# DeltaNet and a mixture of experts on one core: states summed in PSUM and copied by ScalarE, fewer residual and y banks, logits reduced one place later

## Chip, cores and metric

The kernel runs on one NeuronCore of one Trainium2 chip. The metric is the device time of one execution in microseconds (us), lower is better. The kernel before has a median of 526.48 us in 3 runs (524.97 to 529.17).

## The reference

Two layers, one after the other, all in float32. The first is a delta rule over 4 batches, 8 heads, 768 tokens and a head size of 48; the second sends each of its 3072 rows (8 heads x 48 = 384 numbers) through one of 8 experts.

```python
def _attn_ref(q, k, v, beta):
    k_n = k / (np.linalg.norm(k, axis=-1, keepdims=True) + 1e-06)
    state = np.zeros((B, H, D, D))
    for t in range(S):
        y[:, :, t] = np.einsum('bhd,bhde->bhe', q[:, :, t], state)
        v_old = np.einsum('bhde,bhd->bhe', state, k_n[:, :, t])
        state = state + beta[:, :, t] * np.einsum('bhd,bhe->bhde', k_n[:, :, t], v[:, :, t] - v_old)

def _moe_ref(x, w_gate, w1, w2):
    logits = x @ w_gate
    expert_idx = np.argmax(logits, axis=1)
    gate_w = softmax(logits)[np.arange(N), expert_idx]
    for e in range(E):
        mask = expert_idx == e
        out[mask] = gate_w[mask] * (np.maximum(x[mask] @ w1[e], 0.0) @ w2[e])
```

## The kernel before

**Chunks and steps.** The sequence of a batch is cut into 6 blocks of 128 tokens, so there are 24 chunks (block, batch), numbered n = 4 * block + batch. Within a chunk the delta rule is solved in four sub-blocks of 32 tokens. The main loop (L994) is a pipeline over both: step t works on sub-block 0 of chunk t, sub-block 1 of chunk t-1, sub-block 2 of chunk t-2 and sub-block 3 of chunk t-3, all four on the 128 partitions of one tile. It has 27 steps; a step is about 8 us long in the stretch that matters here.

**What a step issues, in this order.** `residual(t)`: TensorE forms in one PSUM bank `ks` what the state (L424) and the solved sub-blocks `u` (L436) predict for the 32-row values, and VectorE subtracts that from the values `v_all` (L443, called the subtraction below). Then, where there are any, four pairs of key products `pg` (L266). Then the last part of the chunk finished in the step before: TensorE forms the rows `xp` of x with their logits (L516), ScalarE copies the row to SBUF (L517), VectorE sums the logits `rl` (L518). Then `apply(t)`: 32 small matmuls of the subtracted values with the inverses `wt` of the sub-blocks (L451), written into the same bank `ks`, which ScalarE copies to `u` (L455, four copies). Then `finish(t-3)`: outputs `yp` from the state (L474), the chunk's key-value product `ku` (L483) which VectorE adds to the state tile `st` in SBUF (L487, two adds), the rest of `yp` (L492), and ScalarE's two copies `yt` (L496). Last, query-key products `pq` (L266), copied by ScalarE and masked by GpSimd (`pm`, L276 and L277). `scale_v(t+1)` scales the next values: on ScalarE for steps 4 to 19 (L404, eight instructions, one per head), on VectorE in the other steps (L407, one instruction).

**Work beside the path.** `beside(t, 0)` to `beside(t, 6)` stand between these parts. Each issues some instructions of the 32x32 inverses on VectorE (L384, L388), of weight splitting for the experts (L695), and of generators on the list `fine`, which give each finished row a slot in its expert's buffer. For chunks below 16 the generator is `pool_slots` (mostly GpSimd), from 16 on `emit_slots` (VectorE). It takes two chunks at a time: `rl` gives an arg-max mask `oh_all` (L635), TensorE counts rows before it with two constant matrices (`pp`, L639 and L642), ScalarE copies the counts (`ct`, L645), GpSimd makes slot numbers `sli` (L660) and issues two scattering DMAs to DRAM (`xg`, L666; in `emit_slots` L582 and L589). Each engine takes its instructions strictly in the order in which this loop issued them, so an instruction that waits holds up all that stands behind it on its engine.

**PSUM before.** The 8 banks are three of tag "y" (`yp`, `ku`, `xp`, `pp`, `db`), two of tag "ks" and three of tag "g".

**After the attention.** Expert 0's rows are read back from `xg` (`xr`, L731), transposed by TensorE (`xt`, L784) and sent through the two expert matmuls (L759, L770); the first of this begins inside the last steps of the loop, and from about 300 us on only the experts are left.

## Time and profile before

| | us |
|---|---|
| median of 3 runs | 526.48 |
| lowest and highest | 524.97, 529.17 |
| profiled execution | 525.89 |
| its span in the trace | 524.2 |

Times of the trace count from the start of the span; what lies outside it is 1.7 us. The mean granted TensorE clock of the span was 0.955. In a row of the trace "[0.64 <-DVE v_all L443]" means that the engine stood idle for 0.64 us before this instruction and that the named instruction released it. PE is TensorE, DVE VectorE, ACT ScalarE, POOL GpSimd, SP SyncE. In the windows, the granted clock is the third column from the right, 1.00 being 2.4 GHz.

### The profile page before, as it was taken

The page shows a single profiled execution, that of the slowest core. Times are in us where ns is not written, and L with a number is a line of the kernel's source. Part 1 is how long each engine was busy: PE and PEld are TensorE (multiplying, and loading weights), DVE is VectorE, ACT ScalarE, POOL GpSimd, SP SyncE. Part 2 cuts the span into 40 slices and gives each one's busy share as a digit, 9 for nine tenths or more (in the row PEclk, how much of TensorE's full clock was granted, in tenths as well). Part 3 has the DMA queues.
Part 4 walks back from the last instruction along what each step waited for, and adds up shares of the span by engine and source line. Part 5 has one row for each costly group of instructions (what it writes and reads, how often), then busy time and mean ns, then how long its engine had stood idle before and what let it go on. Part 6 is the DMA issues. An engine that isn't in the chain of part 4 may idle for free. (4 is left out here: it accounts for less than half of the span.)

```text
span 524.2 us, 17557 instructions
## 1 busy us (share of the span) xinstructions
PE 463.6 (88%) x7212; PEld 426.7 (81%) x7212; DVE 331.6 (63%) x996; ACT 269.5 (51%) x622; POOL 142.9 (27%) x305
## 2 busy tenths in 40 slices
PE   6866769899888888988789999999999999999995
PEld 4755658788776767777689889999999999999995
DVE  3989999698897689435654386636372827445330
ACT  2542236588676667755644246535354636354320
POOL 7002011465763655433130201020202020110202
PEclk9976689899999899898999999999999999999998
DMA  5878769569479557394442156555373636453001
GB/s 165 194 256 227 232 153 315 168 157 294 119 198 275 183 159 225 123 301 123 151 157 80 67 158 221 177 168 160 123 226 114 211 129 210 137 163 108 33 3 44
DMA packets 66060, 87.88 MB, mean 168 GB/s; under 512 B 26425, under 2 KB 50767, under 8 KB 65968
## 3 DMA queue, kind: packets, MB, share of 16 engines
q1 hardware_dynamic: 62512, 77.01, 50.2%
q0 software_dynamic: 3456, 9.57, 5.0%
q8 instruction: 67, 1.10, 0.9%
q14 instruction: 25, 0.20, 0.1%
HBM read 60.24 MB, written 23.56 MB: 160 GB/s over the span
## 5 line engine op out<-in xcount | busy, mean ns | idle before, releaser
L770 PE MATMUL y<-w2h,hx 128*128 128x384 f32 x352 | 93.8, 341 | 0.4 <-PEq L1143 0.4
L773 POOL DMA_INDIRECT out_dram<-yo,idx x32 | 30.7, 958 | 202.3 <-ACT yo L1116 129.8
L695 DVE TENSOR_TENSOR w2l<-w2r,w2h 128x768 fp32r<-128x768 f32 x32 | 31.2, 978 | 69.9 <-ACT w2h L694 69.7
L388 DVE TENSOR_TENSOR lw<-lw,tmp 128x84 f32<-128x84 f32 (+29 forms) x239 | 67.3, 316 | 0.4
L384 DVE TENSOR_TENSOR tmp<-lg,lw 128x84 f32<-128x84 f32 (+29 forms) x239 | 65.2, 307 | 2.5
L770 PEld LDWEIGHTS y<-w2h,hx 128*128 128x128 f32 x352 | 64.1, 188 | 0.7 <-issue 0.7
L455 ACT COPY u<-ks 32x384 f32<-32x384 f32 x96 | 45.1, 470 | 32.8 <-PE ks L451 30.3
L770 PE MATMUL y<-w2l,hx 128*128 128x384 f32 x176 | 59.4, 337 | 0.0
L759 PE MATMUL h<-xl,w1h 128*128 128x384 f32 (+1 forms) x168 | 57.5, 342 | 0.2 <-DVE xl L695 0.2
L759 PE MATMUL h<-xh,w1h 128*128 128x384 f32 (+1 forms) x168 | 57.5, 342 | 0.0
L759 PE MATMUL h<-xh,w1l 128*128 128x384 f32 (+1 forms) x168 | 57.4, 342 | 0.0
L762 ACT ACTIVATE hx<-h 128x448 fp32r<-128x448 f32 (+1 forms) x64 | 32.9, 518 | 33.1 <-PE h L759 32.3
L424 PE MATMUL ks<-st,kt 128*32 128x96 f32 x768 | 46.2, 257 | 2.4 <-issue 2.4
L1116 ACT ACTIVATE yo<-y,gt 128x384 f32<-128x384 f32 x21 | 12.2, 582 | 66.9 <-PE y L770 51.0
L763 DVE SCALAR_TENSOR_TENSOR hx<-h,hx 128x448 fp32r<-128x448 f32 (+1 forms) x64 | 36.9, 587 | 15.1 <-ACT hx L762 14.9
L277 POOL TENSOR_SCALAR_AFFINE_SELECT pm<-pm 128x1024 f32<-128x1024 f32 x24 | 26.6, 1110 | 71.2 <-ACT pm L276 68.6
L451 PE MATMUL ks<-v_all,wt 32*32 32x48 f32 x1536 | 25.7, 206 | 21.6 <-DVE v_all L443 18.9
L249 ACT COPY gg<-pg 128x512 f32<-128x512 f32 x48 | 25.8, 588 | 35.2 <-PE pg L266 35.2
L451 PEld LDWEIGHTS ks<-v_all,wt 32*32 32x32 f32 x1536 | 21.5, 107 | 26.0 <-DVE v_all L443 21.7
L424 PEld LDWEIGHTS ks<-st,kt 128*32 128x32 f32 x768 | 34.5, 113 | 5.8 <-issue 2.9
L266 PE MATMUL pq<-qt,kt 64*128 64x128 f32 x384 | 32.1, 299 | 2.3 <-issue 1.0
L695 DVE TENSOR_TENSOR w1l<-w1r,w1h 128x1024 fp32r<-128x1024 f32 x24 | 29.4, 1225 | 6.8 <-ACT w1h L694 6.8
(194 smaller groups left out, 987.9 us busy)
## 6 DMA issues: line engine op xcount, KB each, us to landing
w1r<-in_w_dram SPq DMA_DIRECT2D x24, 512.0 KB, 4.0
w2r<-in_w_dram SPq DMA_DIRECT2D x32, 384.0 KB, 3.7
kt<-in_kt_dram SPq DMA_DIRECT2D x24, 256.0 KB, 2.8
qt<-in_qt_dram SPq DMA_DIRECT2D x24, 256.0 KB, 5.8
xg<-zrow SPq DMA_DIRECT2D x7, 788.0 KB, 6.2
kg<-in_kt_dram SPq DMA_DIRECT2D x17, 256.0 KB
xr<-xg SPq DMA_DIRECT2D x7, 591.0 KB, 5.2
xn<-row SPq DMA_DIRECT2D x10, 394.0 KB, 5.1
```

Of the source, the lines that this page charges most:

```text
L266: nc.tensor.matmul(pg[a][:, p], lhsT=kt[r, p], rhs=xt[r, p], start=True, stop=True, tile_position=(64 * a, 0), skip_group_check=True)
L384: nc.vector.tensor_tensor(out=x, in0=lg[:, r0:r1, c:c + 1].broadcast_to([128, r1 - r0, b - a]), in1=lw[:, c:c + 1, a:b].broadcast_to([128, ...
L388: nc.vector.tensor_tensor(out=lw[:, r0:r1, a:b], in0=lw[:, r0:r1, a:b], in1=x, op=ALU.add)
L424: nc.tensor.matmul(ks[32 * q:32 * q + 32, 2 * p:2 * p + 2, :], lhsT=kt_t[n % KTL][:, p, 32 * q:32 * q + 32], rhs=st_view(n % B, p), start= ...
L451: nc.tensor.matmul(ks[r, h, :], lhsT=tiles[n // B]["wt"][r, n % B * H + h, :], rhs=vn[r, h, :], start=True, stop=True, tile_position=(32 * ...
L455: nc.scalar.copy(out=uview(n)[r], in_=ks[r])
L695: nc.vector.tensor_tensor(out=lo, in0=src, in1=hi.bitcast(F32), op=ALU.subtract)
L759: nc.tensor.matmul(ps, lhsT=w[:, d, fs], rhs=x_[:, d], start=(n == 0), stop=(n == len(terms) - 1))
L762: nc.scalar.activation(out=hh, in_=ps, func=AF.Relu)
L763: nc.vector.scalar_tensor_tensor(out=hl, in0=ps, scalar=0.0, in1=hh.bitcast(F32), op0=ALU.max, op1=ALU.subtract)
L770: nc.tensor.matmul(ps, lhsT=h(f)[h_], rhs=w2[w][:, f, :], start=(n == 0), stop=(n == len(terms) - 1))
L773: nc.gpsimd.indirect_dma_start(out=out, out_offset=bass.IndirectOffsetOnAxis(ap=idx, axis=0), in_=yo, in_offset=None, bounds_check=N - 1, ...
```

## The change

1. **States as running sums.** `ku` gets no bank of its own any more. Two PSUM banks `sum0` and `sum1` hold the sums of batches 0, 1 and 2, 3 through the whole loop; the matmuls of `ku` add onto them, and only the first ones of block 0 set the start flag. Where VectorE added `ku` to `st`, ScalarE now copies the sum to `st` (two copies of 48x192). The fourth `u` copy is issued ahead of them.
2. **Banks.** The two sum banks come from tag "ks" (2 to 1) and tag "y" (3 to 2). The tiles `db` of batches 2 and 3, used at the start, borrow the sum banks.
3. **Scaling.** `scale_v` runs on VectorE in steps 4 to 10 too; ScalarE keeps steps 11 to 19.
4. **Logits.** The reduction to `rl`, and with it the start of the slot generator, is issued behind `beside(t, 1)` instead of ahead of it. `xp` and the row copy stay where they were.

```diff
-    YB = 3
-    KSB = 2
+    YB = 2
+    KSB = 1
+    VA = 11
...
         if not last:
-            ku = pss.tile([112, NP, D], F32, name=f"ku{tb}_{b}", tag="y", bufs=YB)
+            if tb == 0 and b % 2 == 0:
+                sum_t.append(pss.tile([112, 2, NP, D], F32, name=f"sum{b // 2}", tag=f"sum{b // 2}"))
+            ku = sum_t[b // 2][:, b % 2]
...
                 nc.tensor.matmul(ku[64 * (h % 2):64 * (h % 2) + m, h // 2, :], lhsT=kn, rhs=u[:, h, :],
-                                 start=True, stop=True, skip_group_check=True)
+                                 start=(tb == 0 and b % 2 == 0 and h < 2), stop=True, skip_group_check=True)
             for a in range(2):
                 r = slice(64 * a, 64 * a + D)
-                nc.vector.tensor_tensor(out=st[r, :, r], in0=st[r, :, r], in1=ku[r], op=ALU.add)
+                nc.scalar.copy(out=st[r, :, r], in_=ku[r])
...
-        emit_x(n, yt, row[:, n % w], rl[:, n % w])
+        xp = emit_x(n, yt, row[:, n % w])
+        yield
+        nc.vector.tensor_reduce(out=rl[:, n % w], in_=xp[:, :, 2 * D:].rearrange("t p e -> t e p"), axis=AX.X, op=ALU.add)
         if n % w == w - 1:
             fine.append((pool_slots if n < PG else emit_slots)(tb, b - w + 1, w, row, rl))
...
         beside(t, 0)
         chunk(ks_, t)
         run(fin)
-        if t + 1 < NN + LAG and not B <= t < NN - B:
+        if t + 1 < NN + LAG and not VA <= t < NN - B:
             scale_v(t + 1)
         if t + 1 < NN:
             clear_u(t + 1)
         beside(t, 1)
+        run(fin)
         copies = apply(t)
...
         beside(t, 2)
+        run(copies)
         run(fin)
-        run(copies)
-
-        if B <= t < NN - B:
+
+        if VA <= t < NN - B:
             scale_v(t + 1, act=True)
```

**What moves on TensorE.** Step 14, the counting matmuls `pp` of two chunks and the rows `xp` (`ks`<-`u` is the end of the residual, `ks`<-`v_all` the start of apply). Before:

```order
L436 MATMUL ks_3311<-u_2594,gg_109 32x48
L639 LDWEIGHTS ltri
L639 MATMUL pp_0_3359<-oh_all,ltri 128x16
L642 LDWEIGHTS ones
L642 MATMUL pp_0_3359<-oh_all,ones 128x8
L642 LDWEIGHTS ones
L642 MATMUL pp_0_3359<-oh_all,ones 128x8
L642 LDWEIGHTS ones
L642 MATMUL pp_0_3359<-oh_all,ones 128x8
L516 MATMUL xp_2_3376<-esel,yt_2_3282 128x104 x4
L451 MATMUL ks_3311<-v_all,wt_2772 32x48 x3
```

After:

```order
L523 MATMUL xp_2_3303<-esel,yt_2_3224 128x104 x4
L646 LDWEIGHTS ltri
L646 MATMUL pp_0_3316<-oh_all,ltri 128x16
L649 LDWEIGHTS ones
L649 MATMUL pp_0_3316<-oh_all,ones 128x8
L649 LDWEIGHTS ones
L649 MATMUL pp_0_3316<-oh_all,ones 128x8
L649 LDWEIGHTS ones
L649 MATMUL pp_0_3316<-oh_all,ones 128x8
L454 MATMUL ks_3253<-v_all,wt_2714 32x48 x3
L454 MATMUL ks_3253<-v_all,wt_1905 32x48
```

`pp`, which waits for `oh_all`, stood ahead of `xp` and now stands behind it, right ahead of apply. In steps 6, 8 and 10 the key products `pg` stand between them too, and `pp` moves behind both.

**What moves on VectorE in a step.** Step 16, behind the subtraction: inverse work (`lw`, `tmp`), the logits `rl` and the adds to `st`. Before:

```order
L384 TENSOR_TENSOR tmp_14_3746<-lg_2583,lw_1933 128x51
L518 TENSOR_REDUCE rl_0_3765<-xp_0_3766 128x8
L388 TENSOR_TENSOR lw_1933<-lw_1933,tmp_14_3746 128x17x12
L388 TENSOR_TENSOR lw_1933<-lw_1933,tmp_14_3746 128x17x3
L384 TENSOR_TENSOR tmp_15_3777<-lg_2583,lw_1933 128x192
L384 TENSOR_TENSOR tmp_15_3777<-lg_2583,lw_1933 128x64
L388 TENSOR_TENSOR lw_1933<-lw_1933,tmp_15_3777 128x16x12
L388 TENSOR_TENSOR lw_1933<-lw_1933,tmp_15_3777 128x16x4
L384 TENSOR_TENSOR tmp_16_3835<-lg_2583,lw_1933 128x180
L384 TENSOR_TENSOR tmp_16_3835<-lg_2583,lw_1933 128x75
L487 TENSOR_TENSOR st_135<-st_135,ku_1_3838 48x4x48 x2
L388 TENSOR_TENSOR lw_1933<-lw_1933,tmp_16_3835 128x15x12
```

After:

```order
L387 TENSOR_TENSOR tmp_14_3686<-lg_2521,lw_1907 128x51
L391 TENSOR_TENSOR lw_1907<-lw_1907,tmp_14_3686 128x17x12
L391 TENSOR_TENSOR lw_1907<-lw_1907,tmp_14_3686 128x17x3
L387 TENSOR_TENSOR tmp_15_3701<-lg_2521,lw_1907 128x192
L387 TENSOR_TENSOR tmp_15_3701<-lg_2521,lw_1907 128x64
L511 TENSOR_REDUCE rl_0_3690<-xp_0_3691 128x8
L391 TENSOR_TENSOR lw_1907<-lw_1907,tmp_15_3701 128x16x12
L391 TENSOR_TENSOR lw_1907<-lw_1907,tmp_15_3701 128x16x4
L387 TENSOR_TENSOR tmp_16_3768<-lg_2521,lw_1907 128x180
L387 TENSOR_TENSOR tmp_16_3768<-lg_2521,lw_1907 128x75
L391 TENSOR_TENSOR lw_1907<-lw_1907,tmp_16_3768 128x15x12
L391 TENSOR_TENSOR lw_1907<-lw_1907,tmp_16_3768 128x15x5
```

The reduction `rl` stands four inverse instructions later, and the two adds to `st` are gone.

**What moves on VectorE late.** Step 22, the slot numbers `sli` of chunks 16 and 17 and the subtraction (`w1l` is weight splitting). Before:

```order
L574 TENSOR_REDUCE sl_all<-pos_0_4769 128x2
L582 CAST sli_0_4802<-sl_all 128x2
L695 TENSOR_TENSOR w1l_4612<-w1r_2_4468,w1h_4611 128x1024
L443 TENSOR_TENSOR v_all<-v_all,ks_4809 128x384
L518 TENSOR_REDUCE rl_2_4855<-xp_2_4856 128x8
L407 TENSOR_TENSOR v_all<-v_all,nt_all 128x384
```

After:

```order
L581 TENSOR_REDUCE sl_all<-pos_0_4714 128x2
L702 TENSOR_TENSOR w1l_4544<-w1r_2_4404,w1h_4543 128x1024
L446 TENSOR_TENSOR v_all<-v_all,ks_4740 128x384
L589 CAST sli_0_4782<-sl_all 128x2
L410 TENSOR_TENSOR v_all<-v_all,nt_all 128x384
L511 TENSOR_REDUCE rl_2_4786<-xp_2_4787 128x8
```

The cast to `sli` stood ahead of the weight split and the subtraction, and now stands behind both.

On ScalarE the two `st` copies stand behind the four `u` copies of each step and ahead of the eight scalings and the `yt` copies.

## Rows read from the trace of the kernel before

**Rows 1.** Windows of the span: PE busy (count), PEld, DVE, ACT, POOL, clock, DMA

```profile
60.00:80.00 20.00, 13.78 (x335) 12.02 (x331) 19.61 (x82) 7.35 (x16) 3.38 (x6) 0.77 0.75 207
...
100.00:120.00 20.00, 20.00 (x594) 17.50 (x590) 18.79 (x64) 17.60 (x56) 13.24 (x32) 1.00 0.65 172
...
180.00:200.00 20.00, 17.43 (x542) 14.95 (x539) 17.82 (x63) 13.97 (x45) 9.84 (x24) 1.00 0.62 186
...
300.00:400.00 100.00, 97.38 (x592) 95.55 (x592) 60.28 (x117) 51.19 (x89) 13.37 (x20) 1.00 0.55 171
```

**Rows 2.** Waits of PE, 85 to 260 us: us in total, times, longest

```profile
PE ks L451 <- DVE v_all L443: 5.5, 8, 1.4
PE pp L639 <- POOL oh_all L635: 4.5, 3, 2.1
```

**Rows 3.** Timeline of PE, apply in steps 12, 15, 16, 17, 18

```profile
157.25 0.54 PE L451 MATMUL ks<-v_all,wt 32*32 32x48 f32 x32 [0.35 <-DVE v_all L443]
...
185.02 0.58 PE L451 MATMUL ks<-v_all,wt 32*32 32x48 f32 x35 [0.64 <-DVE v_all L443]
...
194.13 0.56 PE L451 MATMUL ks<-v_all,wt 32*32 32x48 f32 x33 [0.81 <-DVE v_all L443]
...
201.23 0.46 PE L451 MATMUL ks<-v_all,wt 32*32 32x48 f32 x24 [0.27 <-DVE v_all L443]
...
209.54 0.66 PE L451 MATMUL ks<-v_all,wt 32*32 32x48 f32 x42 [1.39 <-DVE v_all L443]
```

**Rows 4.** Timeline of DVE, up to the subtraction of step 16

```profile
190.64 0.47 DVE L388 TENSOR_TENSOR lw<-lw,tmp 128x120 f32<-128x120 f32 x2
...
191.57 1.39 DVE L388 TENSOR_TENSOR lw<-lw,tmp 128x228 f32<-128x228 f32 x2
...
193.52 0.56 DVE L443 TENSOR_TENSOR v_all<-v_all,ks 128x384 f32<-128x384 f32 x1
```

**Rows 5.** Timeline of POOL, the same time

```profile
191.69 1.23 POOL L277 TENSOR_SCALAR_AFFINE_SELECT pm<-pm 128x1024 f32<-128x1024 f32 x1 [1.74 <-ACT pm L276]
```

**Rows 6.** Groups of instructions by line, costliest first

```profile
L404 ACT ACTIVATE v_all<-v_all,nt_all 128x48 f32<-128x48 f32 x128 | 30.5, 319 | 0.0
...
L496 ACT COPY yt<-yp 128x256 f32<-128x256 f32 x48 | 15.1, 357 | 3.1 <-PE yp L492 3.0
L487 DVE TENSOR_TENSOR st<-st,ku 48x192 f32<-48x192 f32 x40 | 14.0, 350 | 11.3 <-PE ku L483 11.0
...
L407 DVE TENSOR_TENSOR v_all<-v_all,nt_all 128x384 f32<-128x384 f32 (+3 forms) x12 | 6.6, 550 | 0.1
```

**Rows 7.** Timeline of PE, pp in steps 10 and 14

```profile
139.44 0.17 PE L639 MATMUL pp<-oh_all,ltri 128*128 128x16 bf16 x1 [2.06 <-POOL oh_all L635]
...
174.94 0.17 PE L639 MATMUL pp<-oh_all,ltri 128*128 128x16 bf16 x1 [2.04 <-POOL oh_all L635]
```

**Rows 8.** Windows of 4 us around step 18, columns as in rows 1

```profile
208.00:212.00 4.00, 2.10 (x82) 1.73 (x80) 3.63 (x17) 1.07 (x3) 2.76 (x12) 0.84 0.43 147
212.00:216.00 4.00, 4.00 (x66) 3.37 (x61) 0.70 (x2) 3.80 (x14) 1.09 (x1) 0.73 0.48 141
```

**Rows 9.** Timeline of ACT, step 17

```profile
195.08 1.95 ACT L455 COPY u<-ks 32x384 f32<-32x384 f32 x4 [1.24 <-PE ks L451]
...
198.76 0.61 ACT L496 COPY yt<-yp 128x256 f32<-128x256 f32 x2
```

**Rows 10.** Timeline of PE, steps 16 and 17

```profile
198.17 0.86 PE L424 MATMUL ks<-st,kt 128*32 128x96 f32 x24
...
199.82 1.14 PE L516 MATMUL xp<-esel,yt 128*128 128x104 f32 x8
```

**Rows 11.** Timeline of DVE, step 22

```profile
245.68 0.54 DVE L443 TENSOR_TENSOR v_all<-v_all,ks 128x384 f32<-128x384 f32 x1
```

**Rows 12.** Timeline of POOL and then of PE, late

```profile
244.84 1.78 POOL L589 DMA_INDIRECT xg<-row,sli  x1 [0.16 <-issue]
...
257.40 0.41 PE L784 MATMUL xt<-ident,xr 128*128 128x128 f32 x2 [1.45 <-DMA xr<-xg]
```

More of the change, by code (lines that the diff above doesn't have):

```diff
@@ L178, in deltanet_moe @@
     st_t = [lp.tile([128, NP, 128], F32, name=f"st{b}") for b in range(B)]
+    sum_t = []
     def clear():
@@ L235, in kpart @@
             db = [psg_[-1].tile([128, NP, 32], F32, name=f"db{b}_0", tag="g"),
-                  pss.tile([128, NP, 32], F32, name=f"db{b}_1", tag="y", bufs=YB)]
+                  pss.tile([128, NP, 32], F32, name=f"db{b}_1", tag="y", bufs=YB) if b < 2 else
+                  pss.tile([128, NP, 32], F32, name=f"db{b}_1", tag=f"sum{b - 2}")]
             for h in range(H):
@@ L510, in st_view, with emit_x @@
         return bass.AP(tensor=t.tensor, offset=t.offset, ap=[list(t.ap[0]), [64, 2], [1, D]])
-    def emit_x(n, yt, row, rl):
+    def emit_x(n, yt, row):
         xp = pss.tile([128, NP, 2 * D + E], F32, name=f"xp{n // B}_{n % B}", tag="y", bufs=YB)
@@ L517, in emit_x @@
         nc.scalar.copy(out=row[:, 0:DM].rearrange("t (p c) -> t p c", p=NP), in_=xp[:, :, 0:2 * D])
-        nc.vector.tensor_reduce(out=rl, in_=xp[:, :, 2 * D:].rearrange("t p e -> t e p"), axis=AX.X, op=ALU.add)
+        return xp
     def emit_slots(tb, b, w, row, rl):
@@ L1038, in deltanet_moe @@
     i = 0
-    run(fin)
+    run(fin, 2)
     while fine:
```

## The prediction

> **What bounds the kernel now.** I first read the windows of the span, to see which engine is full in which stretch. Around 60 to 80 us VectorE is busy 19.61 of 20 us and TensorE 13.78: the first steps are VectorE's. At 100 to 120 us TensorE has no gap at all (20.00 of 20). At 180 to 200 us TensorE is busy 17.43 and VectorE 17.82: they hand work to each other, and neither is full. From 300 us on TensorE is at 97% with the experts alone [rows 1]. So what the change does can count in three places: in the first steps, in the hand-overs between about 120 and 260 us, and at the seam to the experts, where anything won earlier can be lost again at one late load.
>
> Then I read the waits of TensorE from 85 to 260 us. Two kinds stand out: apply waits for VectorE's subtraction, 8 times, 5.5 us; the counting matmuls `pp` wait for GpSimd's mask, 3 times, 4.5 us [rows 2]. The timeline shows where: apply waited 0.35, 0.64, 0.81, 0.27 and 1.39 us in steps 12, 15, 16, 17 and 18 [rows 3]; `pp` waited 2.06 us in step 10 and 2.04 us in step 14 [rows 7], which leaves 0.4 us for the third.
>
> Why is the subtraction late? VectorE works through its queue in order. Ahead of the subtraction of step 16 stands a pair of inverse instructions that took 1.39 us, where a smaller pair just before took 0.47 us; the subtraction then started at 193.52 us [rows 4]. GpSimd's masking of `pm` ran from 191.69 us for 1.23 us, over the same time [rows 5]. So VectorE is behind by a backlog, and the slowed pair adds to it.
>
> **The change, part by part.** Durations come from the profiled execution of 525.89 us; the median is 0.6 us above it, so I work out a difference and take it from the median.
>
> *The adds to the state.* VectorE loses 40 adds of 0.350 us, 14.0 us in all, a pair of 0.70 us a step [rows 6]. Before they could run they waited for `ku`, 11.0 us in all [rows 6], and all inverse work stood behind them. That wait goes too. In the first steps it helps little: the first add is that of step 3. In steps 12 to 18 the backlog ahead of the next subtraction shrinks by at least the pair itself. I let each step win back no more than 0.70 us: 0.35 + 0.64 + 0.70 + 0.27 + 0.70 = 2.7 us. If the lost wait counts as well, all five go: 3.5 us. Lower bound 0, if the slowed pairs of inverse work set the subtraction alone. What is late next is ScalarE (below).
>
> *The copies that replace them.* ScalarE gains 48x192 copies, which the trace of before doesn't show. The nearest row is `yt`: 128x256 in 0.357 us, two in a row in 0.61 us [rows 6, 9]. With fewer elements I take 0.30 us each, 0.5 us a pair; bounds of a pair 0.3 and 0.71 us. They stand ahead of `yt`, and `yt` releases `xp` of the next step. In step 17 `yt` ended at 198.76 + 0.61 = 199.37 us and `xp` began at 199.82 us [rows 9, 10]: a slack of 0.45 us. So in this step, among the shortest, `xp` would wait 0.05 us, at the upper bound 0.26 us. I charge 0.1 us over the two or three steps that are so tight, at most 0.6 us.
>
> *The single bank for residuals.* The first residual matmul of a step now waits until the last `u` copy of the step before has read the bank. In step 16 those copies ended at 195.08 + 1.95 = 197.03 us, and the next residual began at 198.17 us [rows 9, 10]. This 1.14 us is the cover, and the fourth copy stays ahead of the new state copies. Cost 0; without the cover every 0.1 us of lateness costs 0.1 us in each of some 20 steps, since all of TensorE's queue stands behind. Two y banks instead of three: `ku` has left them, and what each next tile waits for is done before apply ends. Cost 0, by the same reading.
>
> *Scaling on VectorE in steps 4 to 10.* Seven instructions of 0.550 us, 3.9 us, go to VectorE; seven sets of eight at 0.319 us leave ScalarE [rows 6]. Each 0.55 us takes the place of 0.70 us of adds in the same step, and at 100 to 120 us TensorE had no gap to win or lose [rows 1]. Cost 0; bounds -0.5 and +1. What speaks against it is the slowed pair: two-input work of VectorE beside GpSimd's masking took 1.39 us [rows 4, 5]. The Trainium skill (GPSIMD Engine Reference, Specifications) says that GpSimd shares SBUF interfaces with VectorE and that VectorE's instructions with two SBUF inputs contend for them. By that rule the scaling (two SBUF inputs) can be slowed where the add, with one input in PSUM, could not. The trace of before agrees for inverse work and shows no scaling beside masking; by the rule up to 0.9 us, the difference of the two pairs, could come on top in some of seven steps.
>
> *Logits and `pp` one place later.* The reduction now finds its row ready, which is part of the 2.7 us. On TensorE `pp` moves behind `xp`, whose eight matmuls take 1.14 us [rows 10], so in a first late round 1.14 us of the wait would be covered. But `pp` starts a chain of its own: counts, slot numbers, two scattering DMAs, and behind them on GpSimd's queue the next mask. If that chain sets the pace, it starts 1.14 us later, the next `pp` is also 1.14 us later in the queue, and the waits of about 2.0 us stay. I credit 0.5 us; bounds -1.1 (one place lost) and 4.5 (all three waits gone).
>
> *The clock.* After the 1.39 us wait of step 18 the granted clock was 0.84 and then 0.73 in two windows of 4 us [rows 8], the lower of two levels (1.2 instead of 2.4 GHz) in part of the time. That cost 4 x 0.16 + 4 x 0.27 = 1.7 us. With half of that wait gone I credit half, 0.9 us; bounds 0 and 1.7.
>
> *The late load.* In step 22 the cast to `sli` moves behind a weight split and the subtraction. The subtraction ended at 245.68 + 0.54 = 246.22 us [rows 11]; with the cast of some 0.2 us and about 0.2 us to the DMA's start, the first scattering DMA would start at 246.6 us where it started at 244.84 us [rows 12]. Its rows are read back for expert 0, and the first transpose already waited 1.45 us for them [rows 12]. So 1.8 us of whatever was won is given back there.
>
> Sum: 2.7 + 0.5 + 0.9 - 0.1 - 1.8 = 2.2 us faster. The profiled execution would be 523.7 us, the median 526.5 - 2.2 = 524.3 us.
>
> **The rivals.**
>
> *More goes than I credit.* All five subtraction waits, all waits for the mask and the whole clock loss: 3.5 + 4.5 + 1.7 - 1.8 = 7.9 us, 518.6 us. For it: VectorE loses waits as well as work. Against it: the mask hangs on DMAs, which no engine's relief makes shorter.
>
> *The gain is absorbed.* GpSimd's chain, then the late load, set the time: what VectorE gives is waited away at `pp` in step 14, only steps 15 to 18 count (2.3 us), and 1.8 us go at the late load: 0.5 us, 526.0 us. For it: the two waits of 2 us. Against it: there are only two of them.
>
> *Slower: the slot chain.* If the rounds of slot numbers are what paces steps 6 to 18, then `pp` behind `xp` makes each round longer by 1.14 us, with nothing left behind `pp` to cover it but apply. Five rounds: 5.7 us, and 1.8 us at the late load, less 2.7 us: 4.8 us slower, 531.3 us. It decides from the point where `pp` waits in every round and not in two or three. For it: the chain is long and late already. Against it: the place of the next `pp` moves by as much.
>
> *The banks do not carry it.* With one bank for residuals TensorE waits at the start of every step once the `u` copies come over 1.14 us later than now. Small waits then repeat, and each fall of the clock like that of step 18 costs 1.7 us: four of them, with the 0.9 us not won, make 524.3 + 0.9 + 6.9 = 532.1 us. The change would then not do what it says, since freed VectorE time only turns into waits for banks. The Trainium skill (TensorE: Matmul & The Clock Gate, A second HAM failure mode: psum-queue depth-cycling) describes this: a kernel that cycles through PSUM banks idles briefly between groups of matmuls, and the clock swings. By that rule this rival decides. The trace of before shows falls of the clock behind waits for other engines; no row of it shows one behind a wait for a bank.
>
> **How the numbers follow.** Forecast 0.48, more 0.20, absorbed 0.17, slot chain 0.10, banks 0.05. The median of few executions moves by about 1% for no reason, 5.3 us, so "faster" means below 521.2 us: the case of more, and a tenth of the forecast's, where most bounds fall well: 0.25. "Slower" means above 531.8 us: most of the banks' case, half of the slot chain's, and a little for what I have not seen: 0.13. The same: 0.62. The range reaches down to 517.5 us, 1 us below the case of more, and up to 530 us, short of the two slow cases.
>
> **What would show it.** Right: no apply waits of over 0.7 us for the subtraction in steps 12 to 18; copies to `st` near 0.3 us on ScalarE; `pp` still waiting in steps 10 and 14; about 3 us of wait ahead of the first transpose; no wait of the first residual matmul for a `u` copy. Wrong: waits for `u` copies or `yt` in most steps, a mean granted clock well under 0.955 with `pp` waiting in every round, or no wait for the mask at all.

## The result, and the profile after

| | before | after |
|---|---|---|
| median of 22 runs each, us | 527.32 | 534.12 |
| lowest and highest, us | 521.54, 533.77 | 526.86, 540.13 |
| ratio after to before | | 1.0123, 95% interval 1.0093 to 1.0154 |
| profiled execution, us | 525.89 | 535.3 |
| its span, us | 524.2 | 532.9 |
| mean granted TensorE clock | 0.955 | 0.939 |

The change makes the kernel slower by 1.2%, about 6.5 us; the forecast was 2.2 us faster. The ratios leave the long executions of either kernel out, and the profile shown is one taken in a further run of the changed kernel, because its first profile fell on a long execution.

The page's first part, of the changed kernel: engine, busy us, share of the span, instructions.

```profile
PE 462.3 (87%) x7212; PEld 426.5 (80%) x7212; DVE 320.6 (60%) x963; ACT 271.9 (51%) x606; POOL 145.7 (27%) x305
```

The change does what it says. VectorE has 33 instructions fewer (40 adds less, 7 scalings more) and 11.0 us less work, and TensorE is as busy as it was (462.3 against 463.6 us). Its idle time is 10 us longer, 70.6 instead of 60.6 us, so in this profile the loss is in waits.

Groups by line, of the changed kernel (busy us, mean ns of one, idle just before them and what ended most of it):

```profile
L407 ACT ACTIVATE v_all<-v_all,nt_all 128x48 f32<-128x48 f32 x72 | 17.2, 321 | 0.2
L501 ACT COPY yt<-yp 128x256 f32<-128x256 f32 x48 | 15.8, 375 | 4.0 <-PE yp L497 3.5
...
L492 ACT COPY st<-sum 48x192 f32<-48x192 f32 x40 | 12.4, 310 | 1.0 <-PE sum L488 0.6
...
L410 DVE TENSOR_TENSOR v_all<-v_all,nt_all 128x384 f32<-128x384 f32 (+3 forms) x19 | 10.4, 549 | 0.1
```

These answer to [rows 6]. The copy that took the place of the adds costs 310 ns, against the 0.30 us that I had estimated, and a scaling on VectorE costs 549 ns, as before (550 ns). The prices of the operations were right.

Waits of TensorE in the changed kernel, 85 to 265 us: what waits and for what, us in total, times, longest.

```profile
PE pp L646 <- POOL oh_all L642: 8.9, 3, 6.6
PE ks L454 <- DVE v_all L446: 4.0, 2, 2.6
PE yp L477 <- ACT ct L652: 2.8, 2, 2.6
PE ks L454 <- issue: 2.8, 4, 1.4
PE xt L791 <- DMA xr<-xg: 1.7, 1, 1.7
```

Against [rows 2]: apply waits for the subtraction 2 times instead of 8, and both are late (step 22 and behind it), so in steps 4 to 20 that wait is gone, as forecast. But the mask costs 8.9 us instead of 4.5, and a wait that did not exist, of the outputs `yp` for the counts `ct`, has 2.8 us.

Timeline of TensorE in the changed kernel, the places of these waits (start, us, instruction, the wait ahead of it):

```profile
124.31 0.67 PE L477 MATMUL yp<-qt,st 64*64 64x128 f32 x16 [2.58 <-ACT ct L652]
...
180.18 0.17 PE L646 MATMUL pp<-oh_all,ltri 128*128 128x16 bf16 x1 [6.55 <-POOL oh_all L642]
```

Its windows of 4 us around the second of these, with the columns of [rows 1]:

```profile
176.00:180.00 4.00, 0.00 (x0) 0.00 (x0) 3.04 (x16) 0.48 (x1) 2.85 (x12) 0.66 0.27 103
180.00:184.00 4.00, 3.82 (x105) 3.35 (x106) 2.15 (x7) 2.06 (x6) 3.37 (x12) 0.50 0.01 4
```

TensorE did nothing for 6.55 us, and came back to a granted clock of 0.50, the lower level (1.2 GHz), for the next 4 us. What `pp` waited for is on GpSimd's timeline in the same kernel:

```profile
164.09 1.11 POOL L673 DMA_INDIRECT xg<-row,sli  x1 [0.60 <-POOL sli L667]
...
170.31 1.01 POOL L673 DMA_INDIRECT xg<-row,sli  x1 [2.56 <-DMA xg<-row,sli]
...
176.32 0.70 POOL L342 COPY nt_all<-r 32x32 f32<-32x32 f32 x3 [4.48 <-DMA xg<-row,sli]
...
179.81 0.32 POOL L642 TENSOR_SCALAR oh_all<-oh 128x16 bf16<-128x16 f32 x1
```

The two scattering DMAs of a pair of chunks run one behind the other, some 6 us each: the second waits for the semaphore that tells of the first one's landing, and the copies of the norms (`nt_all`), in the queue ahead of the next mask, wait for that of the second. A round of slot numbers, from the `pp` of step 12 to the mask of step 14, takes 21.3 us here and 19.2 us in the profile of before.

### The profile page after: what moved, and what is told of

It reads as the page before. It is cut to its first block, busy times and chain, and to the rows that moved or that the text cites. A ratio compares the mean times of both kernels' runs of the same rounds, so it can differ in the third digit from the quotient of the medians.

```text
span 534.4 us, 17510 instructions
## 1 busy us (share of the span) xinstructions
PE 468.8 (88%) x7212; PEld 430.9 (81%) x7212; DVE 318.9 (60%) x963; ACT 271.9 (51%) x606; POOL 153.6 (29%) x305
## 5 line engine op out<-in xcount | busy, mean ns | idle before, releaser
L391 DVE TENSOR_TENSOR lw<-lw,tmp 128x84 f32<-128x84 f32 (+29 forms) x239 | 64.2, 303 | 0.2
L427 PE MATMUL ks<-st,kt 128*32 128x96 f32 x768 | 48.0, 264 | 4.4 <-issue 2.3
L280 POOL TENSOR_SCALAR_AFFINE_SELECT pm<-pm 128x1024 f32<-128x1024 f32 x24 | 30.8, 1282 | 69.1 <-ACT pm L279 66.5
L454 PE MATMUL ks<-v_all,wt 32*32 32x48 f32 x1536 | 27.5, 211 | 21.4 <-DVE v_all L446 18.8
L454 PEld LDWEIGHTS ks<-v_all,wt 32*32 32x32 f32 x1536 | 22.9, 111 | 25.1 <-DVE v_all L446 20.3
L446 DVE TENSOR_TENSOR v_all<-v_all,ks 128x384 f32<-128x384 f32 (+3 forms) x28 | 15.4, 550 | 44.9 <-PE ks L439 29.6
L427 PEld LDWEIGHTS ks<-st,kt 128*32 128x32 f32 x768 | 35.6, 117 | 6.0 <-ACT u L458 2.6
```

The source lines that it names most:

```text
L280: nc.gpsimd.affine_select(out=pm, in_=pm, compare_op=ALU.is_gt, fill=0.0, base=0, pattern=[[0, H], [1, C]], channel_multiplier=-1)
L391: nc.vector.tensor_tensor(out=lw[:, r0:r1, a:b], in0=lw[:, r0:r1, a:b], in1=x, op=ALU.add)
L427: nc.tensor.matmul(ks[32 * q:32 * q + 32, 2 * p:2 * p + 2, :], lhsT=kt_t[n % KTL][:, p, 32 * q:32 * q + 32], rhs=st_view(n % B, p), start= ...
L454: nc.tensor.matmul(ks[r, h, :], lhsT=tiles[n // B]["wt"][r, n % B * H + h, :], rhs=vn[r, h, :], start=True, stop=True, tile_position=(32 * ...
```

## The experiments

All ratios are to the kernel before, run beside on the same chip; the experiments ran on four chips, so a small difference between two ratios can be one of the chips. One profile is one execution, and the stretch between the subtractions of steps 4 and 20 has a length between 134 and 150 us over all profiles, whatever the edit. So single profiles prove little there: I compare means over groups of kernels.

**The changed kernel once more.**

> The changed kernel once more, for a second profile and more times. In its first profile ScalarE's row copy of step 8 waited 2.9 us for the second scattering DMA of an earlier pair, the counts copy and the u copies stood behind it, and TensorE waited 2.4 us ahead of yp. Theory 1 (GpSimd's memset ahead of that DMA): the same chain is there again, TensorE waits 2 to 3 us at that yp, and the kernel is 5 to 8 us slower than before. Rival (the clock by chance alone, or ScalarE's load): no such wait in this profile, with the time still 5 to 8 us slower.

Measured: 1.0213 (1.0140 to 1.0286), in six runs. The wait is there again (2.58 us); the loss, 10 to 11 us, is larger than expected. The 22 runs behind the 1.0123 above are others, and the two intervals just overlap.

**Part 4 alone, and all but part 4.** In the changed kernel:

```diff
         xp = emit_x(n, yt, row[:, n % w])
-        yield
         nc.vector.tensor_reduce(out=rl[:, n % w], ...)
```

> The changed kernel with only part 4 undone: the logits are reduced and the slot generator starts in the old place, so the DMA stands ahead of the memset, and pp and its counts copy ahead of xp and the row copy. Theory 1: the wait in step 8 goes, and the time is 526 to 529 us, at least 4 us under the changed kernel. Rival (banks: one for residuals, two of y): TensorE waits for y tiles or u copies as before, time within 2 us of the changed kernel.

And part 4 alone in the kernel before (the same `yield` put in, with the second `run(fin)` of the change):

> The kernel before with part 4 alone: logits and slot generator one place later, banks, adds and scaling as before. Theory 1: GpSimd has the same order, memset ahead of the DMA, so the row copy waits in step 8 and the u copies behind it; with a third y bank TensorE waits at ku rather than at yp; 2 to 5 us slower than before. Rival (banks): no slower than before, 525 to 528 us.

Measured: without part 4 1.0047 (0.9988 to 1.0106); part 4 alone 1.0154 (1.0090 to 1.0218). By these ratios most of the loss hangs on the place of the logits, and parts 1 to 3 are not a gain to which part 4 does harm. How much hangs on it is less sure: the twelve times without part 4 lie between 522.52 and 541.93 us, and their median, 531.09 us, is only 3.5 us under that of the changed kernel beside it (534.59), with 524.21 for the kernel before. The expected 526 to 529 us was missed. So was the 2 to 5 us for part 4 alone, some 8 us by its ratio, of which the wait in step 8, at `ku` as expected, is 1.2 us.

**Which chunks?** Part 4 undone for the last 8 chunks only (in the changed kernel), and done for these alone (in the kernel before):

```diff
         xp = emit_x(n, yt, row[:, n % w])
-        yield
+        if n < PG:
+            yield
```

> The changed kernel with part 4 undone for the last 8 chunks alone (steps 20 on); the first 16 keep the later place. Theory 2 (the later place costs in steps 20 to 26, by the late load of expert 0 and the late counts): from the subtraction of step 20 to that of step 26 about 60 us where the changed kernel takes 64, no wait ahead of the first transpose over 1.5 us, and 3 to 5 us under the changed kernel. Rival (the later place costs in the first 16 chunks, by memset, row copy and counts): under 1.5 us from the changed kernel.

```diff
-        emit_x(n, yt, row[:, n % w], rl[:, n % w])
+        xp = emit_x(n, yt, row[:, n % w])
+        if n >= PG:
+            yield
+        nc.vector.tensor_reduce(out=rl[:, n % w], ...)
```

> The kernel before with part 4 for the last 8 chunks alone. Theory 2: 4 to 6 us more from step 20 to step 26, and 3 to 5 us (0.6 to 1.0%) slower than before. Rival (the first 16 chunks): within 1.5 us of before.

Measured: 1.0048 (0.9997 to 1.0100) and 1.0070 (1.0029 to 1.0110). Undoing it for 8 chunks leaves the same ratio as undoing it for all 24, so for the first 16 no cost of the place of the logits shows. The profile with part 4 alone agrees: from step 4 to 20 it took 134.7 us, among the shortest, and from step 20 to 26 65.8 us, the longest of all. But part 4 alone cost 1.5% for all chunks and 0.7% for the late ones, in intervals that barely overlap, so a cost in the first 16 isn't excluded. VectorE's timeline in the kernel with the late chunks alone moved, step 22:

```profile
246.16 0.55 DVE L443 TENSOR_TENSOR v_all<-v_all,ks 128x384 f32<-128x384 f32 x1
246.63 0.16 DVE L585 CAST sli<-sl_all 128x2 int32<-128x2 f32 x1
```

And in the changed kernel with the late chunks put back:

```profile
241.04 0.17 DVE L590 CAST sli<-sl_all 128x2 int32<-128x2 f32 x1
...
242.27 0.55 DVE L446 TENSOR_TENSOR v_all<-v_all,ks 128x384 f32<-128x384 f32 x1
```

The first late scattering DMA started 0.91 us behind the start of the subtraction in the former (247.07 us) and 0.78 us ahead of it in the latter (241.49 us); in the kernel before it was 0.84 us ahead [rows 11, 12]. So it comes 1.75 us later, as the forecast had worked out. Those of the next pairs come later still, in part because the steps themselves have become longer: the third one started 17.9 us behind the subtraction of step 22 in the kernel before, and 23.1 us behind it with the late chunks alone moved. The time it costs is more than the first shift. The stretch from the subtraction of step 20 to that of step 26 as one window, columns as in [rows 1], in the kernel before:

```profile
225.08:284.47 59.39, 50.72 (x1165) 43.92 (x1163) 31.92 (x94) 30.98 (x70) 17.09 (x23) 0.97 0.51 161
```

and with the late chunks alone moved:

```profile
226.23:289.73 63.50, 53.79 (x1167) 46.66 (x1164) 32.74 (x95) 31.10 (x70) 16.00 (x23) 0.92 0.46 150
```

The same matmuls; TensorE idles 9.7 instead of 8.7 us, and its busy time is 3.1 us longer at a clock of 0.92 instead of 0.97. The four profiles of kernels with the later place have 63.5 to 65.8 us here, mean 64.2 (the changed kernel's first profile, not among them, 64.3); the thirteen with the old place (all others but the one without adds and the last one, below) 58.8 to 61.8, mean 60.7. Of these 3.5 us, 1.7 are idle time and 1.8 longer busy time at the lower clock (mean 0.91 against 0.95). The 3.5 us are 0.67% of the time, where the run measured 0.70%. One of the added waits is plain in TensorE's timeline in step 25, here of the changed kernel and then, the same matmul, of the kernel before:

```profile
285.51 0.18 PE L559 MATMUL pp<-oh_all,ltri 128*128 128x8 bf16 x1 [1.01 <-DVE oh_all L555]
```

```profile
278.28 0.17 PE L552 MATMUL pp<-oh_all,ltri 128*128 128x8 bf16 x1
```

All profiles with the later place show this wait of 1.0 us, where the kernel before shows 0.1 us. The wait that the forecast named, ahead of the first transpose `xt`, is longer in the means too (1.8 us in the four profiles, 0.4 in the thirteen). But the loss does not need it: with the late chunks alone moved there was none, where the kernel before waited 1.45 us.

**The wait for `ct`.** In step 8 of the changed kernel one instruction of GpSimd, which clears a buffer, waits 2.34 us for VectorE; the second scattering DMA stands behind it, the copy to `row` on ScalarE waits for that, and `ct`, on which `yp` waits, stands behind the copy. ScalarE's timeline shows the end of that chain:

```profile
123.69 0.48 ACT L524 COPY row<-xp 128x384 f32<-128x384 f32 x1 [3.07 <-DMA qt<-in_qt_dram]
124.07 0.18 ACT L652 COPY ct<-pp 128x24 f32<-128x24 f32 x1
```

The trace names another DMA as the releaser of the copy to `row`. That it was the scatter of the row buffer is my reading. In the kernel with part 4 alone, at the same place, the trace names the scatter itself:

```profile
122.60 0.48 ACT L519 COPY row<-xp 128x384 f32<-128x384 f32 x1 [1.87 <-DMA xg<-row,sli]
```

The edit tests what the chain costs: in the changed kernel, the clearing is issued six places later.

```diff
-            clear_w(tb + 3)
+            if tb + 3 < NT - 1:
+                clear_w(tb + 3)
+            else:
+                later.append([place[0] + 6, tb + 3])
...
+        while later and later[0][0] <= place[0]:
+            clear_w(later.pop(0)[1])
```

> The changed kernel with one instruction moved: GpSimd's memset of the third inverse tile comes 6 places later, behind the second scattering DMA. Theory 1: the row copy of step 8 no longer waits for a DMA, yp does not wait for the counts copy, and the time is 3 to 6 us under the changed kernel. Rival (the later place itself, pp behind xp, costs the time in many steps): nothing but that wait goes, under 2 us.

Measured: 1.0166 (1.0094 to 1.0239). The wait in step 8 is gone, and one of 1.6 us stands in step 12. Beside the changed kernel's 1.0213 in the same group that is 2 us or so less, well within the intervals, and under the 3 us that the theory wanted. So the chain was read rightly, and most of the loss is not in it.

**Is it the norms' copies?** They wait behind the scattering DMAs, ahead of the mask. VectorE writes the norms directly, in both kernels (parts 1 to 3 for the first of them):

```diff
-        if tb > 0:
-            nc.vector.transpose(out=s1, in_=s0)
...
-            if tb > 0:
-                nc.gpsimd.tensor_copy(nt_t[p, c], s1[p])
-            else:
-                nc.vector.transpose(out=nt_t[p, c], in_=s0[p])
+            nc.vector.transpose(out=nt_t[p, c], in_=s0[p])
```

> The changed kernel without part 4, and with the copies of the norms for blocks 1 to 5 done by VectorE (transposes straight to their place) instead of GpSimd, so that nothing between the second scattering DMA and the next mask waits for that DMA. If the time that VectorE gave back is waited away at pp of step 14, that wait (5.6 us without part 4) falls under 1 us, and the kernel is 3 to 6 us faster than without part 4, 1 to 4 us faster than before. If the wait is there only by a late start of the round, it stays and the time stays.

> The kernel before with the copies of the norms on VectorE. Its wait at pp of step 14 was 2.0 us; if the copies cause it, it goes, and the kernel is 1 to 3 us faster than before; otherwise the same within 1 us.

Measured: 1.0068 (1.0027 to 1.0109) and 0.9986 (0.9953 to 1.0018). In the kernel before, the waits for the mask between steps 4 and 20 fell from 4.5 to 0.3 us, those for the subtraction rose from 3.8 to 5.3, and the time is the same. In the kernel with parts 1 to 3 the wait at the `pp` of step 14 fell from 5.6 to 1.4 us, and its ratio is not lower than the 1.0047 without this edit. So taking away waits for the mask brought nothing that can be measured in either kernel.

**Do VectorE's adds cost anything?** The kernel before without them:

```diff
-            for a in range(2):
-                r = slice(64 * a, 64 * a + D)
-                nc.vector.tensor_tensor(out=st[r, :, r], in0=st[r, :, r], in1=ku[r], op=ALU.add)
```

> The kernel before without VectorE's adds to the state (the states stay zero, so what the chunks after the first hand on is left out): VectorE has all the relief of the change, ScalarE no new work, banks as before. If VectorE's relief is worth what I forecast: the subtraction's waits in steps 12 to 18 go and the kernel is 2.5 to 5 us faster. Theory 3 (TensorE's waits for the mask, and its waits without a cause in the profile, take their place): the waits for the subtraction fall under 1.5 us, the other waits grow by 2 us or more, and the time is within 1 us of before.

The states stay zero in this kernel, so rows go to other experts: it took 680.8 us (ratio 1.2926), and of its time only the attention's stretch says something. Waits of TensorE in it, 86 to 226 us:

```profile
PE ku L483 <- issue: 4.2, 2, 2.2
PE pp L636 <- POOL oh_all L632: 3.5, 3, 2.2
PE ks L424 <- issue: 2.0, 1, 2.0
PE ks L451 <- issue: 1.9, 3, 0.9
```

No wait for the subtraction is left, and the stretch from step 4 to 20 takes 138.4 us instead of 139.3, inside its scatter. What went came back as waits that the profile gives no cause for ("issue"), 12.3 us instead of 7.1; the last section says what these go with. So freeing VectorE, the main gain of the forecast, shows no gain beyond the scatter even with nothing put in the adds' place. It is one profile, and in a scatter of 134 to 150 us it can't tell a gain of 2.7 us from none.

**Parts 1 to 3, piece by piece.** Each is one edit. States as sums and the banks, with the scaling as before (in the changed kernel without part 4):

```diff
-    VA = 11
+    VA = B
```

> Part 1 and 2 alone: sums in PSUM copied by ScalarE, one residual bank, two y banks; scaling on ScalarE in steps 4 to 19 and logits in the old place, as before. Theory 3 (the relief of VectorE is not worth anything here, since TensorE's next wait takes its place): within 0.5% of before. Rival (banks or ScalarE's copies cost time): 2 to 4 us slower than before. Rival (the scaling of part 3 is what costs): as fast as or faster than before, and 2 to 4 us under the changed kernel without part 4.

The scaling alone (kernel before), where the change's `VA` is 11:

```diff
-        if t + 1 < NN + LAG and not B <= t < NN - B:
+        if t + 1 < NN + LAG and not 11 <= t < NN - B:
...
-        if B <= t < NN - B:
+        if 11 <= t < NN - B:
```

> The kernel before with part 3 alone: seven scalings moved from ScalarE to VectorE, 3.9 us of VectorE's time. Theory 3: within 0.5% of before. If scaling beside GpSimd's masking is what costs: instructions of L407 well over 0.55 us, and 2 to 4 us slower than before.

All scaling on VectorE (changed kernel without part 4, `VA = 24`):

> The changed kernel without part 4, with all scalings on VectorE (ScalarE loses 1.9 us in each of steps 11 to 19, VectorE gains 0.55 us). Theory 4: the round from pp of step 12 to the mask of step 14 falls from 22 to about 19 us, the wait at pp of step 14 under 3 us, and the time 1 to 4 us under the kernel without part 4. Rival (the round is long for another reason): the round stays over 21 us and the time within 1 us.

One residual bank alone (kernel before):

```diff
-    KSB = 2
+    KSB = 1
```

> The kernel before with one residual bank instead of two, all else as it was. Theory 3 and my reading of the 1.14 us of cover: no wait of the first residual matmul for u copies from step 4 on, waits of 0.3 to 1.1 us in steps 1 to 3 hidden behind VectorE, the same time within 0.5%. Rival (banks): 2 us or more slower.

One residual bank and two y banks, with `ku` in two of its own:

```diff
-    YB = 3
-    KSB = 2
+    YB = 2
+    KSB = 1
...
-            ku = pss.tile([112, NP, D], F32, name=f"ku{tb}_{b}", tag="y", bufs=YB)
+            ku = pss.tile([112, NP, D], F32, name=f"ku{tb}_{b}", tag="ku", bufs=2)
```

> The kernel before with the change's banks alone: one residual bank, two y banks, and the two banks that this frees given to ku; adds on VectorE, scaling and logits as before. If the smaller rotation costs time (it is what the changed kernel with copies by VectorE shares with the one with copies by ScalarE, both 0.5 to 0.7% slower): 0.4 to 0.8% slower, with waits of yp or xp for a y bank (named by the counts copy or by yt). If not: within 0.3% of before, as one residual bank alone was (0.28%, -0.1 to 0.7).

The sums copied by VectorE (changed kernel without part 4):

```diff
-                nc.scalar.copy(out=st[r, :, r], in_=ku[r])
+                nc.vector.tensor_copy(st[r, :, r], ku[r])
```

> The changed kernel without part 4, its copies to st made by VectorE instead of ScalarE: ScalarE has no new work, VectorE keeps 40 instructions. If ScalarE's copies are what costs (yt late, xp waits 0.2 to 0.3 us in several steps): no waits of xp for yt under step 20, and 1 to 3 us faster than without part 4. Theory 3: within 1 us of it.

Two copies of the same size put on ScalarE at the same place, with the adds kept (kernel before, run twice):

```diff
                 nc.vector.tensor_tensor(out=st[r, :, r], in0=st[r, :, r], in1=ku[r], op=ALU.add)
+                nc.scalar.copy(out=yt[r, :, 0:D], in_=tiles["ks", n + LAG][r, 0:NP, :])
...
         beside(t, 2)
-        run(fin)
         run(copies)
+        run(fin)
```

> The kernel before with two more ScalarE copies of 48x192 in each chunk, where the st copies of the change stand (behind the four u copies); they read the residual bank and write a part of yt that is written again at once, so the result is the same. Nothing else changes: adds on VectorE, banks and logits as before. Theory 4 (ScalarE's copies make the masking and the counts late, GpSimd's rounds of slot numbers get longer): from pp of step 8 to the mask of step 10, and from pp of step 12 to the mask of step 14, about 21 us instead of 19; waits at pp together over 6 us; 2 to 4 us slower than before. Rival (ScalarE has room): rounds of 19 us, waits at pp of 2 to 4.5 us, within 1 us of before.

> The same kernel as in the run before it with ScalarE's extra copies, once more, since that run was 0.95% slower (0.53 to 1.38) while its profile showed rounds of 19.5 us and less waiting in all than before. If ScalarE's copies cost time: 0.5 to 1.3% slower again. If that was chance: within 0.5% of before.

| kernel | ratio | 95% interval | medians of all runs, this and before, us |
|---|---|---|---|
| sums and banks, old scaling | 1.0069 | 1.0022 to 1.0115 | 530.22, 525.47 |
| scaling as changed, alone | 1.0049 | 1.0007 to 1.0091 | 528.23, 525.47 |
| sums, all scaling on VectorE | 1.0131 | 1.0078 to 1.0184 | 531.28, 526.91 |
| one residual bank | 1.0028 | 0.9991 to 1.0066 | 526.51, 525.47 |
| one residual, two y banks | 1.0054 | 1.0014 to 1.0095 | 528.35, 528.03 |
| sums copied by VectorE | 1.0071 | 1.0034 to 1.0108 | 528.08, 525.47 |
| copies added on ScalarE | 1.0095 | 1.0053 to 1.0138 | 529.56, 526.91 |
| the same again | 1.0054 | 1.0009 to 1.0099 | 528.59, 528.03 |

Every piece is 0.3 to 1.3% slower by its ratio, 0.1 to 0.9% by the medians, and none is a gain. But for the lowest and the highest, one residual bank and all scaling on VectorE, their intervals overlap, so they can't be told apart. All kernels with parts 1 and 2, and the old place for the late chunks, stand at 1.005 to 1.007, but for the one with all scaling on VectorE. There the round came down to 19.5 us and the wait at the `pp` of step 14 to 1.7 us, as theory 4 had it, and the kernel was not faster for it. One residual bank does in three early steps what the prediction had excluded (the expectation ahead of this run allowed it), TensorE's waits from 45 to 86 us in that kernel:

```profile
PE ks L451 <- DVE v_all L443: 13.9, 4, 6.5
...
PE ks L424 <- ACT u L455: 2.0, 3, 1.0
```

The second row is the wait for the bank: 2.0 us in three steps, in a stretch that is VectorE's in any case [rows 1], and none later.

The table of the means shows where the states as sums lose what they win. Waits of TensorE between the subtractions of steps 4 and 20:

| us | 10 kernels with adds | 7 with ScalarE's copies |
|---|---|---|
| waits for the subtraction | 3.2 | 0.2 |
| waits for the mask | 3.1 | 7.1 |
| waits without a cause | 7.7 | 8.0 |
| idle time of TensorE | 15.8 | 18.0 |
| length of the stretch | 138.9 | 142.7 |

(The kernel without adds, the one that copies with VectorE and the changed kernel's first profile are in neither column; the lengths scatter by 3 to 4 us within each.) The 3 us that were to go went, and the mask took 4. The rounds of slot numbers tend to be longer: from the `pp` of step 12 to the mask of step 14 17.3 to 22.6 us in the seven kernels with ScalarE's copies, 15.8 to 19.8 us in the ten with the adds. ScalarE's mere load does not do that: with the added copies the rounds are 19.5 and 18.8 us. Those copies wait for nothing, while the real ones wait for `ku`; whether that is it was not tried, and stays open. Nor is the longer wait for the mask bound to ScalarE: with the sums copied by VectorE it was 7.1 us, in a round of 19.1 us, in its one profile.

**Starting the late chain earlier.** If its lateness costs, its earliness should gain. Kernel before, six steps of the generator a place instead of four in the last 4 chunks' steps and behind:

```diff
-        for _ in range(STEPS[i] if t < NN - B else 4):
+        for _ in range(STEPS[i] if t < NN - B else 6):
```

> The kernel before with six instead of four steps of the slot generators in each place from step 20 on: the opposite of the later place in the last 8 chunks, which cost 3.5 us there. If the order of the late slot numbers is what counts: steps 20 to 26 take 57 to 59 us and the kernel is 0.3 to 0.6% faster than before. If what is left there is VectorE's weight splitting: no change.

Measured: 0.9941 (0.9886 to 0.9995), by about 3 us the one version whose interval lies under the kernel before. The stretch from step 20 to 26 takes 58.3 us, the shortest of all profiles. In VectorE's timeline the cast stands 2.2 us ahead of the subtraction:

```profile
246.61 0.17 DVE L582 CAST sli<-sl_all 128x2 int32<-128x2 f32 x1
...
248.82 0.55 DVE L443 TENSOR_TENSOR v_all<-v_all,ks 128x384 f32<-128x384 f32 x1
```

The gain is at the edge of what its interval can tell, and 58.3 us is one profile, 0.5 us under the least of the thirteen. It points the same way as the two others (cast behind the subtraction 64.2 us, ahead of it 60.7), but it is no proof by itself.

## Why the prediction was wrong, point by point

**What held.** The copy's price (310 ns against 0.30 us). The waits for the subtraction: credited 2.7 us, measured 3.0 in the means. The place and size of the first late shift: 1.76 us worked out, 1.75 measured. `pp` still waits in steps 10 and 14. So most signs named for "right" came, and the kernel is slower all the same: they tell that the credited waits went, not that the time went with them. By parts, the forecast had parts 1 to 3 some 3.5 us faster (2.7 - 0.1 + 0.9) and part 4 1.3 us slower (0.5 - 1.8). The runs have parts 1 to 3 about 0.5% (2.5 us) slower, and part 4 0.7% (3.7 us) slower by its late chunks and 1.5% by the run of all of it.

**The adds to the state: right size, wrong worth.** This is the step that failed in the main term: 2.7 us of waits were taken for 2.7 us of time, on the ground that "What is late next is ScalarE". Late next was the mask (+4.0 us in the means); in the kernel without adds it was waits that no releaser explains (12.3 us instead of 7.1). In the middle steps nothing came of the relief that stands out of the scatter. My rival "the gain is absorbed" had this for the middle steps. I had the evidence: at 180 to 200 us neither TensorE nor VectorE is full [rows 1], which speaks for a chain that goes through several engines, and against a queue that is too long. I credited the relief of one link in full.

**The late load: the mechanism was right in part, and its size was off.** I charged 1.8 us, the first shift itself, as a longer wait ahead of the first transpose ("about 3 us"). In the means that wait grew by 1.4 us; in the changed kernel's profile it was 1.75 us, and with only the late chunks moved it was not there, at a loss of 0.7%. The stretch lost 3.5 us. What I left out: the chain has more than one hand-over, so that a second late `pp` waits 1.0 us as well; and TensorE's matmuls in the stretch ran at a lower granted clock, so that beside 1.7 us of idle time stand 1.8 us of longer busy time. That the waits lower the clock is my reading of these means, and it does not hold of each wait: in the kernel with the late chunks alone moved the clock was 0.51 in the 4 us from 247.4 us on, behind a wait of 1.92 us, and 1.00 behind the two waits of 1.0 us for the mask (from 274.8 and 284.6 us). In the forecast's sum I priced the clock as a credit alone.

**The rounds of slot numbers.** "I credit 0.5 us" was wrong in sign for the whole change: the waits for the mask rose. But not for the reason of the rival "the slot chain": that rested on `pp` moved behind `xp`. With part 4 alone the waits for the mask between steps 4 and 20 were 2.65 us, less than the 4.5 before, and the rounds are as long without part 4 (21.8 us). Its 531.3 us and the 532.1 us of the banks were the numbers nearest to the result. That is luck, as far as the runs show: neither reason was borne out.

**The banks.** "What each next tile waits for is done before apply ends. Cost 0" failed for two y banks with part 4: `yp` waited up to 2.7 us for `ct`, where the counts of a pair now hold the bank. The wait is there in the kernels that have both, and in none that has only one of the two. Delaying what stood at its head gave no clear gain. For one residual bank the cost stayed within 0 to 0.7% by its interval. As it was put, the rival "the banks do not carry it" falls: no row shows `u` holding up a residual in most steps. But the banks alone, one residual and two y, stand at 1.0054 (1.0014 to 1.0095), as much as parts 1 to 3 lose, though the medians of all runs are 0.3 us apart; so a cost of the banks that shows in no single wait is not excluded.

**The clock.** Of the 0.9 us credited nothing came. The mean granted clock went from 0.955 to 0.939.

**The scaling on VectorE.** With seven scalings moved the cost can't be separated from the rest; with all of them moved the kernel was the slowest of the pieces (1.0131), and why is open. By the Trainium skill (GPSIMD Engine Reference, Specifications) an instruction of VectorE with two SBUF inputs can contend with GpSimd. The inverse work agrees with it: in the slowed pair [rows 4] it is the small instruction, 128x19, that took 1.08 us, against 0.18 to 0.21 us elsewhere in that profile, and over all twenty profiles the updates of `lw` took over 0.55 us in 114 of 344 cases beside the masking and in none of 4436 others. For the scaling the runs decide little. In the steps from 4 on none stood beside the masking when all of them were on VectorE, and of two that did in the changed kernel (119.4 and 130.5 us) neither was slowed (544 and 548 ns); one ahead of the main loop's steps, at 24.0 us of the changed kernel without part 4, took 969 ns beside it.

The sum as the runs have it: 0.7% (3.5 us) for the late place, and about 0.5% (2.5 us) for parts 1 to 3, makes 1.2%, and the 1.23% measured agrees. In the group of the 1.0213 it is 1.5% for part 4 alone and 0.5% for the rest, which makes 2.0%. So the two shares add up in either group, but the size of part 4's share is known only as 0.7 to 1.5%. Open is what parts 1 to 3 lose their 0.5% to: the longer waits for the mask are what the means show, yet two kernels in which the wait at the `pp` of step 14 fell to 1.4 and 1.7 us were not faster, and no single piece carries it.

## What to carry to other kernels

Where no engine is full and several hand work on, price a relief by what waits next in the same chain, not by the waits that go; a run with the work simply left out tells that bound early. Look at long chains with DMAs in them (here scattering rows that are read back) before busy engines: with the start of the chain one place later in the last 8 chunks, so that the cast which releases its first DMA stood behind a subtraction of 0.55 us, the kernel took 0.7% longer, and with the chain issued faster it took some 0.6% less, at the edge of its interval. Where the granted clock falls after a wait of TensorE, charge the wait twice, once as idle time and once as slower matmuls.

## What the runs showed of the hardware that I had not expected

TensorE has waits for which the profile names no releaser, and they recur at the same places of its instruction stream. One stands ahead of a query-key product `pq` of step 20 in all twenty profiles, 1.0 to 3.9 us long. In the kernel before:

```profile
230.93 0.71 PE L266 MATMUL pq<-qt,kt 64*128 64x128 f32 x6 [1.02 <-issue]
```

With one residual bank:

```profile
228.38 0.49 PE L266 MATMUL pq<-qt,kt 64*128 64x128 f32 x5 [2.98 <-issue]
```

Without the adds:

```profile
232.51 0.60 PE L266 MATMUL pq<-qt,kt 64*128 64x128 f32 x5 [2.56 <-issue]
```

They are 7 to 8 us of the stretch between steps 4 and 20 in the means, more than any wait with a name in the kernel before, and 12.3 us in the kernel without adds.

The profile names no engine for them, but the list of DMAs tells what they go with. For 228.5 to 228.6 us in the kernel before, 2.4 us ahead of the end of the first of these three waits, it has a packet of 16 KB on queue q8, which brings instructions:

```profile
q8 instruction: 1, 0.02, 58.2%
```

In the twenty profiles, between 85 and 290 us, TensorE has 198 waits of over 0.3 us without a releaser and 231 with one. Of the former 167 end 2.2 to 3.0 us after a packet of q8 starts, of the latter 30. And 174 of the former stand at every 256th instruction of TensorE's stream (its sequencer's waits counted with the matmuls and weight loads), at the same offset in all profiles, and none of the latter. So the likeliest cause is that TensorE waits there for its next instructions. No run tests it, but it fits that edits of the other engines' work leave these waits standing.

The other was the scatter to DRAM: two of GpSimd's indirect DMAs of one pair of chunks took about 6 us each (164.09, 170.31, 176.32 us), the second waiting for the semaphore of the first, and GpSimd stood still for 2.56 and 4.48 us of it. Its busy time (27% of the span) says nothing of that.
